# An H3 convolution block and squared-ReLU MLP: from a hand-placed order to a recorded graph with a list scheduler

## The chip, the core and the metric

The kernel runs on one NeuronCore of a Trainium2 chip. The metric is the device time of one execution, in microseconds. The core has five engines with an instruction queue each: TensorE (PE, with its weight loads shown as PEld), VectorE (DVE), ScalarE (ACT), GpSimd (POOL) and SyncE (SP), which here only issues DMA transfers. PE writes to PSUM, eight banks of 128 partitions x 512 f32; the other data lie in SBUF.

## What is computed

One block with B = 1, S = 2048 tokens, D = 640 channels, F = 1728 hidden units. Everything is f32.

```
sa, ca, ga, sb, cb, gb = six rows of (silu(c) @ w_mod)
h  = layernorm(q) * (1 + ca) + sa
ks = causal depthwise convolution of k with 4 taps
kv = ks * v
y  = long causal convolution of kv with ssm_k, per channel (FFT of length 4096) + kv * ssm_D
x  = q + ga * (h * y)
h  = layernorm(x) * (1 + cb) + sb
out = x + gb * (relu(h @ w1 + b1)^2 @ w2 + b2)
```

In this kernel the gate `ga` is row 2 of the modulation, folded into the rows for `ca` and `sa`; row 5 (`gb`) and `b2` are folded at the end.

## The kernel before

**Front: the convolution, in five blocks of 128 channels.** For each block `b`:

- `kv_load` brings k and v token-major in four pieces of 512 tokens; PE transposes them (`kv_k`, L236, and `kv_v`, L273) into PSUM; ACT and DVE apply the four taps (L238, L258) and DVE multiplies by v (L280). The product is stored to a scratch tensor `kv_d` in DRAM, and read back in another layout by `load_x` into half of the tile `p`; `load_h` reads `ssm_k` into the other half.
- `unit_a` (L380, tiles `pa`): the first stage of the FFT, 64x64 tiles of PE, four at a time; ACT copies the result to the tile `a`. Each block has eight of them, four for the filter (i = 1) and four for kv (i = 0).
- `front` (L394): the second stage, `spectrum`, for the filter (`h`) and for kv (`x`); DVE multiplies the two (L146) and POOL combines real and imaginary parts (L149, L152). In block 0 the filter's spectra are done ahead by `early_h`.
- `back` (L460, tiles `qp`): the first inverse stage, four groups a block; ACT copies to `QT`.
- `unit_t` (L523) transposes `QT`, and `unit_y` (L532) is the last inverse stage. It contracts 64 rows into 32 columns, one tile for each parity of the token tile, and fills two PSUM banks with 8 of the 16 token tiles:

```python
        for a in range(4):
            for i in range(2):
                l = slice(64 * i, 64 * i + 64)
                pe.matmul(
                    y[i][32 * a : 32 * a + 32].rearrange("p l d -> p (l d)"),
                    ca[l],
                    tss[4 * g + a][l].rearrange("p i d -> p (i d)"),
```

- `prep_a`, `prep_m`, `prep_p` make the normalised and modulated q; `gate` multiplies it with y on DVE (L146, `up<-up,KV`; in block 4 y is multiplied straight out of PSUM, L544). `finish_near` adds the first 512 tokens into the MLP's first two token tiles, `finish_add` adds the rest and stores it to the scratch tensor `x1_d`.

Beside these run the layernorm statistics of q (`stats1`) and the modulation: `part_load`, `part_scale`, `part_add`, and the column sums on PE (`mod_row`, L320; `mod_col`, L347; for row 5 `gate_sum`, L935).

**MLP.** w1 and w2 are split into a high and a low fp32r part (`w_load`, `w_high` on ACT, `w_low` on DVE). Eight tiles of 256 tokens; each runs over 14 groups of hidden units: `mlp_front` (L702; L715 and L729 in the first tile; L706 for the half-size last group), the squared ReLU (L747, L149, L749), a split into high and low (`mlp_split`, L141, L152), and `mlp_back` (L790, tiles `acc`), which runs `MLAG = 3` groups behind.

**What sets the order.** The order of each engine is the order of the calls, kept by `keep_order`. The calls of the front are written by hand: the loop over blocks calls `front`, `back`, `unit_a`, `unit_t` and `unit_y` at slots `FS(b, j)` and `GS(b, s)` listed in `UNITS`, and a table of about 100 `at(...)` lines hangs the other steps on the slots:

```python
    at(FS(1, 8), (stats1, 13), (part_add, 2, 2, pool), (part_load, 1, 0))
    at(GS(1, 1), (load_x, 2), (kv_s, 3, 0), (part_load, 1, 1))
```

All loads and stores but a few go through SP in this order (`sp_dma`, L133); each waits until the fourth one before it has landed (`OUT = 4`). PSUM is divided by tags: X (four banks: `pa`, spectra, later `acc`), Y (two: `qp`, `kt`, `y`, later `xtp`) and T (two: `t`, `mr`, some `kt` and `vt`, later the MLP's `h`).

Of the kernel before, what the change touches and what calls it, by code (L numbers as in the profile page):

```python
# [15 lines left out]
AX_X = mybir.AxisListType.X  # L16
# [5 lines left out]
NG = 16  # L22
# [5 lines left out]
MLAG = 3  # L28
OUT = 4


def _constants():
# [17 lines left out]
    for mm in range(1, 32):  # L50
# [30 lines left out]
        "ca": np.concatenate([ca, ca]).astype(f),  # L81
        "gb": gb.reshape(128, 4096).astype(f),
        "gi": gt.reshape(128, 4096).astype(f),
# [4 lines left out]
def ssm_mlp_kernel(  # L88
# [21 lines left out]
    pe, act, dve, pool, sp = nc.tensor, nc.scalar, nc.vector, nc.gpsimd, nc.sync  # L110


    def keep_order():
        info = mybir.DependencyInfo(mybir.DependencyClass.NoSync, mybir.DependencyReason.DATA)
        engines = {e.engine: None for e in (pe, act, dve, pool, sp)}
        for i in nc.cur_bb.bb.instructions:
            if i.engine in engines:
                if engines[i.engine] is not None:
                    tc.add_manual_dep(i, engines[i.engine], info, reason="order")
                engines[i.engine] = i.name  # L120
# [5 lines left out]
    kv_d = dr.tile([D, S], F32, tag="kv_d", name="kv_d")  # L126
    x1_d = dr.tile([S, D], F32, tag="x1_d", name="x1_d")
# [3 lines left out]

    def sp_dma(o, i):
        sp.dma_start(o, i)  # L133
# [5 lines left out]
    def copy(eng, o, i):  # L139
        if eng is act:  # L140
            act.activation(o, i, AF.Copy)  # L141
        else:
            eng.tensor_copy(o, i)

    def mul(eng, o, a, b):
        eng.tensor_mul(o, a, b)  # L146
# [4 lines left out]
    def sub(eng, o, a, b):  # L151
# [3 lines left out]
    WX = [sb.tile([P, 10, P], F32, tag=f"WX{i}", name=f"wx{i}") for i in range(4)]  # L155
    WE = sb.tile([P, 8, P], F32, tag="WE", name="we")
    HXS = [WX[0][:, 0:4], WX[0][:, 4:8]]
    MS = [(WX[i][:, 0:4], WX[i][:, 4:8]) for i in (1, 3)]
    TS = [WX[i][:, 4 * j : 4 * j + 4] for i in (2, 1, 3) for j in range(2)]
    WS = [  # L160
        (WE[:, 0:2], WE[:, 2:4]),
        (WE[:, 4:6], WE[:, 6:8]),
        (WX[2][:, 8:10], WX[3][:, 8:10]),
        (WX[2][:, 4:6], WX[2][:, 6:8]),
    ]
    cw = WX[0][:, 8].rearrange("p (r n) -> p r n", r=2)
    ca = WX[1][:, 8, 0:32]

    KV = sb.tile([P, 5120], F32, tag="KV", name="KV")
    KACC = [KV[:, 512 * i : 512 + 512 * i] for i in range(2)]  # L170
    KN = [
        KV[:, 1024 + 1024 * i : 2048 + 1024 * i].rearrange("p (w t d) -> p w t d", w=2, t=4)
        for i in range(4)
    ]
    K0 = sb.tile([P, 4, 512], F32, tag="UP1", name="kacc0")
    UT = KV[:, 3072:5120].rearrange("p (l d) -> p l d", l=NL)
    ktail = sb.tile([P, 2, 4], F32, tag="ktail", name="ktail")
    kover = sb.tile([P, 2, 4], F32, tag="kover", name="kover")


    ident = sb.tile([P, P], F32, tag="ident", name="ident")
    make_identity(nc, ident)
    d0 = sb.tile([P, D], F32, tag="STG", name="d0", bufs=4)
    dve.memset(d0, 0.0)
    ones = sb.tile([P, P], F32, tag="ones", name="ones")
    dve.memset(ones, 1.0)
    eps_t = sb.tile([P, 1], F32, tag="eps", name="eps_t")
    dve.memset(eps_t, EPS)
    dsm = sb.tile([P, NB, DG], F32, tag="dsm", name="dsm")
    tap = sb.tile([P, NB, 4], F32, tag="tap", name="tap")  # L190


    hsrc = ssm_k.rearrange("(g a) (n i) -> (a n) g i", a=4, i=64)
    xsrc = kv_d.rearrange("(g a) (n i) -> (a n) g i", a=4, i=64)
    qsrc = q.rearrange("(n c l) d -> c n l d", n=32, c=4)
    osrc = out.rearrange("(n c l) d -> c n l d", n=32, c=4)
    pt = {}

    def p_tile(b):
        pt[b] = sb.tile([P, 2, DG, 64], F32, tag=f"S{b % 2}", name=f"p_{b}")  # L200

    def load_h(b, n=4):
        w = DG // n
        for i in range(n):
            sp_dma(
                pt[b][:, 1, i * w : (i + 1) * w],
                hsrc[:, b * DG + i * w : b * DG + (i + 1) * w, :],
            )

    def load_x(b, n=4):  # L210
        w = DG // n
        for i in range(n):
            sp_dma(
                pt[b][:, 0, i * w : (i + 1) * w],
                xsrc[:, b * DG + i * w : b * DG + (i + 1) * w, :],
            )


    def kv_load(i):
        b, h = divmod(i, 4)  # L220
        rows = slice(h * 512, (h + 1) * 512)
        cols = slice(b * P, (b + 1) * P)
        t = KN[h % (4 if b == 0 else 2)]
        for w, src in ((0, k), (1, v)):
            sp_dma(t[:, w], src[rows, cols].rearrange("(t p) d -> p t d", p=P))

    kt = {}

    def kv_k(b, h, tag="Y"):
        acc = KACC[h % 2] if b else K0[:, h]  # L230
        t = kt[0] = ps.tile(
            [P, 512], F32, tag=tag, name=f"kt_{b}_{h}", bufs=4 if tag == "X" else 2
        )
        kn = KN[h % (4 if b == 0 else 2)]
        for j in range(4):
            pe.transpose(t[:, j * P : (j + 1) * P], kn[:, 0, j], ident)  # L236
        c = 3 if h and b else 0
        act.activation(acc[:, c:], t[:, c:], AF.Copy, scale=tap[:, b, 0:1])  # L238
        if h < 3:

            kl, ko = ktail[:, h % 2], kover[:, h % 2]
            copy(act, kl[:, 0:3], t[:, 509:512])
            if b == 0:
                return
            pool.tensor_scalar(ko[:, 0:3], kl[:, 0:3], tap[:, b, 3:4], None, op0=ALU.mult)
            for o, x, i in ((1, 2, 2), (0, 1, 2), (0, 2, 1)):
                o = ko[:, o : o + 1]
                pool.tensor_scalar(o, kl[:, x : x + 1], tap[:, b, i : i + 1], o, op0=ALU.mult, op1=ALU.add)

    def kv_s(b, h):  # L250
        acc, tk = KACC[h % 2] if b else K0[:, h], kt[0]
        if h and b:
            dve.scalar_tensor_tensor(
                acc[:, 0:3], tk[:, 0:3], tap[:, b, 0:1], kover[:, (h - 1) % 2, 0:3], op0=ALU.mult, op1=ALU.add
            )
        for t in (1, 2, 3):
            o = acc[:, t:]
            dve.scalar_tensor_tensor(  # L258
                o, tk[:, : 512 - t], tap[:, b, t : t + 1], o, op0=ALU.mult, op1=ALU.add
            )  # L260
            if h and b == 0:
                o = acc[:, :t]
                dve.scalar_tensor_tensor(
                    o, ktail[:, (h - 1) % 2, 3 - t : 3], tap[:, b, t : t + 1], o, op0=ALU.mult, op1=ALU.add
                )

    def kv_v(b, h, tag="X"):
        t = kt[1] = ps.tile(
            [P, 512], F32, tag=tag, name=f"vt_{b}_{h}", bufs=4 if tag == "X" else 2
        )  # L270
        kn = KN[h % (4 if b == 0 else 2)]
        for j in range(4):
            pe.transpose(t[:, j * P : (j + 1) * P], kn[:, 1, j], ident)  # L273
        n = 4 * b + h + 2
        if 6 <= n < 4 * NB:
            kv_load(n)

    def kv_m(b, h):
        acc = KACC[h % 2] if b else K0[:, h]
        dve.tensor_mul(acc, kt[1], acc)  # L280
        sp_dma(kv_d[b * P : (b + 1) * P, h * 512 : (h + 1) * 512], acc)


    st1 = sb.tile([P, NL, 2], F32, tag="st1", name="st1")
    rs1 = sb.tile([P, NL], F32, tag="rs1", name="rs1")
    nm1 = sb.tile([P, NL], F32, tag="nm1", name="nm1")

    qt = {}

    def dve_stats(o, t):  # L290
        s6 = sb.tile([P, 2, 6], F32, tag="s6", name="s6", bufs=2)
        for i in range(2):
            dve.bn_stats(s6[:, i], t[:, i * 320 : (i + 1) * 320])
        dve.bn_aggr(o, s6)

    def stats1(l):
        dve_stats(st1[:, l], qt[l])

    def stats1_end():
        act.activation(rs1, st1[:, :, 1], AF.Sqrt, bias=eps_t)  # L300
# [4 lines left out]
    ct = sb.tile([P, NB], F32, tag="ct", name="ct")  # L305
    sg = sb.tile([P, NB], F32, tag="sg", name="sg")
    row0 = sb.tile([P, D], F32, tag="row0", name="s1row")
    row1 = sb.tile([P, D], F32, tag="row1", name="g1row")
    cbs = sb.tile([P, 2, NB], F32, tag="cbs", name="cbs")
# [102 lines left out]

    qn = [0]
    ws = {}


    def front(b, j, early):
        n = qn[0]
# [863 lines left out]
```

## Time and profile before

| | us |
|---|---|
| median of 3 runs | 707.78 |
| the runs | 707.78, 711.22, 707.54 |
| the profiled execution | 713.03 |
| its span, first to last instruction | 711.2 |
| mean granted clock of PE | 0.965 |

The page of the profile gives the span and the busy time of each engine. A view by stretches gives for each stretch its length, the busy time of each engine with the number of instructions, the granted PE clock, the busy share of the 16 DMA engines, and GB/s. A row of the timeline reads: start, duration, engine, line, operation, out<-in, shapes, how many instructions were merged, and in brackets the idle time before it with what ended it. Starts are exact; the ends of matmuls are modelled, so the distance from one start to the next is the better price of a group. A matmul of f32 leaves two records, a transpose one. `SPq` is SP's queue of DMA issues.

### The profile page before, as it was taken

To read this page: it belongs to the slowest core of one execution; us is meant where nothing else is said; L and a number is where in the kernel's file an instruction comes from. 1 tells how busy PE (TensorE), PEld (TensorE's weight loads), DVE (VectorE), ACT (ScalarE), POOL (GpSimd) and SP (SyncE) were. 2 spreads that over 40 slices of the span, in tenths; PEclk is the share of its full clock that TensorE was granted. 3 is DMA by queue.
4 is the path that set the end of the run, shared out by engine and by line. 5 is a ranking of instruction groups with operands and counts; after the bars stand their busy time and mean duration, and the time that the engine had idled before them with its cause. 6 is when DMAs were issued, how large, how long until landed. Compare 5 with 4: busy or idle time off the path is not lost.

```text
span 711.2 us, 18076 instructions
## 1 busy us (share of the span) xinstructions
PE 647.9 (91%) x7589; PEld 583.0 (82%) x7589; DVE 417.2 (59%) x785; ACT 325.3 (46%) x683; POOL 253.0 (36%) x299
## 2 busy tenths in 40 slices
PE   6698499688969978799999999999999999999996
PEld 5687288467748858689999999999999999999995
DVE  5256646647767569768854555464555545555633
ACT  4435355568675786556533323323333333233221
POOL 1052145437966966952520300301302204103301
PEclk9999699989998999999999999999999999999999
DMA  9888977969675176338311020020020110200101
GB/s 231 247 245 197 238 194 204 234 190 214 162 201 150 51 176 151 116 104 242 104 38 38 1 75 1 1 74 1 1 75 1 38 38 1 75 1 1 38 1 38
DMA packets 109125, 74.46 MB, mean 105 GB/s; under 512 B 49266, under 2 KB 96370, under 8 KB 108788
## 3 DMA queue, kind: packets, MB, share of 16 engines
q1 hardware_dynamic: 107088, 72.87, 39.5%
q8 instruction: 60, 0.98, 0.6%
q10 hardware_dynamic: 1892, 0.43, 0.3%
q14 instruction: 21, 0.17, 0.1%
q0 software_dynamic: 64, 0.01, 0.0%
HBM read 58.86 MB, written 14.42 MB: 103 GB/s over the span
## 4 chain that ended last, share of the span: by engine, by line
PE 61%; ACT 4%; DVE 2%; DMA 2%; issue 1%; POOL 1%; DVEq 0%; POOLq 0%; ACTq 0%
PE acc L790 26%; PE h L702 22%; PE h L715 2%; PE x L394 1%; PE h L394 1%; ACT KV L493 1%; PE h L706 1%; PE qp L460 1%; PE y L532 1%; PE xtp L667 1%; DMA xp<-in_A_q_dram 1%; ACT wx L141 1%; PE gr L935 1%; PE t L523 1%; DVE w_S L152 1%
## 5 line engine op out<-in xcount | busy, mean ns | idle before, releaser
L790 PE MATMUL acc<-w_S,hring 128*128 128x320 f32 x960 | 156.7, 311 | 0.2 <-DVE hring L152 0.2
L702 PE MATMUL h<-xt,w_S 128*128 128x512 f32 (+1 forms) x770 | 149.6, 340 | 0.0
L790 PEld LDWEIGHTS acc<-w_S,hring 128*128 128x128 f32 x960 | 144.8, 188 | 4.8 <-DVE hring L152 0.7
L702 PEld LDWEIGHTS h<-xt,w_S 128*128 128x128 f32 x770 | 120.1, 189 | 14.1
L152 DVE TENSOR_TENSOR hring<-mtmp,hring 128x256 fp32r<-128x256 f32 x112 | 67.3, 601 | 69.7 <-ACT hring L141 69.7
L152 POOL TENSOR_TENSOR xt<-we,xt 128x256 fp32r<-128x256 f32 x35 | 27.4, 783 | 201.3 <-ACT xt L141 200.3
L149 DVE TENSOR_TENSOR mtmp<-h,mtmp 128x256 f32<-128x256 f32 (+1 forms) x99 | 41.9, 423 | 96.7 <-ACT mtmp L747 94.1
L747 ACT ACTIVATE mtmp<-h,b1t 128x256 f32<-128x256 f32 x91 | 43.1, 474 | 114.1 <-PE h L702 112.6
L141 ACT ACTIVATE hring<-mtmp 128x256 fp32r<-128x256 f32 x112 | 46.1, 412 | 73.9 <-DVE mtmp L749 63.2
L380 PEld LDWEIGHTS pa<-wx,p 64*64 64x64 f32 x2560 | 48.6, 154 | 23.8 <-issue 16.5
L380 PE MATMUL pa<-wx,p 64*64 64x64 f32 x2560 | 54.1, 242 | 13.6 <-DMA p<-kv_d 6.3
L141 ACT ACTIVATE a<-pa 128x512 f32<-128x512 f32 x80 | 45.2, 633 | 22.7 <-PE pa L380 22.3
L146 DVE TENSOR_TENSOR wx<-x,wx 128x512 f32<-128x512 f32 x64 | 40.8, 683 | 19.4 <-PE x L394 11.0
L394 PE MATMUL x<-a,gb 128*64 128x128 f32 x640 | 44.9, 287 | 5.0 <-DVE wx L146 2.3
L394 PEld LDWEIGHTS x<-a,gb 128*64 128x64 f32 x640 | 38.9, 145 | 6.6 <-PE h L394 3.0
L149 POOL TENSOR_TENSOR wm<-wm,wm 128x640 f32<-128x640 f32 x20 | 31.5, 1577 | 27.9 <-ACT wm L338 27.6
L749 DVE SCALAR_TENSOR_TENSOR mtmp<-mtmp 128x256 f32<-128x256 f32 x91 | 39.6, 435 | 3.1
L258 DVE SCALAR_TENSOR_TENSOR KV<-kt,tap,KV 128x511 f32<-128x511 f32 (+2 forms) x48 | 35.9, 748 | 7.9 <-ACT ktail L141 6.4
L394 PE MATMUL h<-a,gb 128*64 128x128 f32 x512 | 35.9, 284 | 2.7 <-ACT wx L141 2.7
L523 PE MATMUL t<-ident,q 128*128 128x128 f32 x160 | 25.6, 294 | 13.1 <-ACT wx L141 6.8
L394 PEld LDWEIGHTS h<-a,gb 128*64 128x64 f32 x512 | 30.2, 143 | 7.6 <-issue 3.8
L141 ACT ACTIVATE q<-qp 128x512 f32<-128x512 f32 x39 | 21.1, 593 | 32.9 <-PE qp L460 32.9
(151 smaller groups left out, 1082.7 us busy)
## 6 DMA issues: line engine op xcount, KB each, us to landing
wm<-in_w_mod_dram SPq DMA_DIRECT2D x25, 320.0 KB, 4.3
KV<-in_A_k_dram SPq DMA_DIRECT2D x20, 256.0 KB, 4.2
KV<-in_A_v_dram SPq DMA_DIRECT2D x20, 256.0 KB, 4.2
p<-in_A_ssm_k_dram SPq DMA_DIRECT2D x20, 256.0 KB, 4.9
p<-kv_d SPq DMA_DIRECT2D x20, 256.0 KB, 4.5
xp<-in_A_q_dram SPq DMA_DIRECT2D x20, 256.0 KB, 5.3
out_dram<-x SPq DMA_DIRECT2D x28, 160.0 KB, 2.6
w1s<-in_B_w_dram SPq DMA_DIRECT2D x13, 320.0 KB, 4.0
```

The costliest lines, as they stand in the source:

```text
L141: act.activation(o, i, AF.Copy)
L146: eng.tensor_mul(o, a, b)
L149: eng.tensor_add(o, a, b)
L152: eng.tensor_sub(o, a, b)
L258: dve.scalar_tensor_tensor(o, tk[:, : 512 - t], tap[:, b, t : t + 1], o, op0=ALU.mult, op1=ALU.add)
L380: pe.matmul(t[e][64 * r : 64 * r + 64, g].rearrange("p m d -> p (m d)"), pt[b][l, i, 8 * q + g, :], cw[l, r], start=True, stop=True,)
L394: pe.matmul(t[64 * a : 64 * a + 64, s + r], gb[:, g, r, a], AX[b][i][:, 2 * g + a], start=True, stop=True,)
L523: pe.transpose(t[:, i], x, ident)
L702: pe.matmul(*x, start=(b == 0 and x is both), stop=(b == NB - 1 and x is both))
L747: act.activation(r, h[:, 1], AF.Identity, bias=b1t[:, f : f + 1])
L749: dve.scalar_tensor_tensor(r, r, 0.0, r, op0=ALU.max, op1=ALU.mult)
L790: pe.matmul(acc[2 * s + i], h[:, a, s * P : (s + 1) * P], w[:, y, i * 320 : (i + 1) * 320], start=(f == 0 and ti == 0), stop=(f == NF - 1 ...
```

## The change

The kernel's calls no longer issue instructions. They record nodes in a graph, with the buffers that they read and write, a rough cost, and for each buffer the places where it may lie. `Graph.order` then runs a list scheduler in the source: at every moment each engine takes the ready node of highest priority (length of the longest path behind it, plus hand-set offsets by kind and block in `BIAS`) whose buffers find a free place; it keeps account of SP's four transfers in flight, of PE's instruction supply (a matmul counts 4 entries, 256 entries in 4 us), and of a port that DVE and POOL share. `emit` issues the nodes in that order. `FS`, `GS`, `at`, `AFTER`, `UNITS` and `MLAG` go.

```diff
+    def order(self, lag=0.1, pelag=0.2, patience=0.0, trace=None):
...
+                    for k, (pr, i) in enumerate(ready[e]):
+                        if nodes[i].lock and port[0] > t + 1e-9 and port[1] != e:
+                            continue
+                        got = place(nodes[i])
+                        if got is not None:
+                            pick = k
+                            break
...
+                    if e == "PE":
+                        ent += n.entries
+                        if ent >= 256:
+                            end = max(end, block + 4.0)
+                            block, ent = end, ent - 256
...
+    g.bias = BIAS
+    g.emit(g.order())
     keep_order()
```

PSUM is eight single banks; most tiles of the front may take any of them, `qp` any of four, and in the MLP `acc` has banks 0 to 3, `h` and `xtp` banks 4 to 7:

```diff
+    bank = [ps.tile([P, 2, 512], F32, tag=f"PS{i}", name=f"ps{i}") for i in range(4)]
...
+    ANY = (0, 1, 2, 3, 4, 5, 6, 7)
+    ONE = (6, 7)
+    MAIN = (0, 1, 2, 3)
+    SIDE = (4, 5)
...
+    KVB, PAB, XB, QB = ANY[::-1], ANY, ANY, ANY[2:6][::-1]
+    TB, YB, XTB, HB, ACCB = ANY[::-1], ANY[::-1], SIDE + ONE, SIDE + ONE, MAIN
```

The last inverse stage contracts both parities at once. The constant `ca` becomes block diagonal, 128 rows by 64 columns with half of it zeros, `gi` is permuted to suit, and a call of `unit_y` makes one quarter of the tokens (4 of 16 token tiles) in one bank, with two matmuls of 512 columns:

```diff
-        "ca": np.concatenate([ca, ca]).astype(f),
+        "ca": np.kron(np.eye(2), ca).astype(f),
...
+    def unit_y(b, l):
...
+            for h in range(2):
+                mm(
+                    y[64 * h : 64 * h + 64].rearrange("p l d -> p (l d)"),
+                    ca,
+                    ts[h].rearrange("p l d -> p (l d)"),
+                    True,
+                    True,
+                    hold=[d],
+                )
...
+        if raw:
+            copy(act, d, y)
+            mul(dve, d, d, u)
+            U[b, l] = d
+        else:
+            mul(dve, u, y, u)
```

`raw` holds for blocks 0 and 1; in blocks 2 to 4 the product with the normalised q `u` is read straight from PSUM. The products on POOL after the spectra are now in place (`wr` and `wi` lie in `m0`), with a small tile `keep` for the two rows of the first group. The counts of the other matmuls and transposes, the transfers, and the arithmetic of the MLP are those of before.

In the order that results, SP's queue begins with the eight k and v loads of block 0. The reload `load_x` of block 0 is issued as transfers 27 to 30 (20 to 23 before), behind the eight k and v loads and two stores of block 1. The spectra of a block are interleaved with `qp`, `t` and `y` of the block before it:

```
... pa2 pa2 pa2 pa2 pa2 pa2 h2 h2 vt3 x2 x2 vt3 vt3 mr1 y1 h2 x2 t1 t1 kt4 h2 x2 kt4 h2 x2 ...
```

(a name is one group on PE, with its block; `mr1` is the product of modulation row 1). In the MLP's first tile PE runs 45 parts of `mlp_front`, five to a hidden group, ahead of the first part of `mlp_back`.

More of the change, by code (lines that the diff above doesn't have):

```diff
@@ L109, in ssm_mlp_kernel @@
     nc = tc.nc
-    pe, act, dve, pool, sp = nc.tensor, nc.scalar, nc.vector, nc.gpsimd, nc.sync
+    engines = {"PE": nc.tensor, "ACT": nc.scalar, "DVE": nc.vector, "POOL": nc.gpsimd, "SP": nc.sync}
     def keep_order():
         info = mybir.DependencyInfo(mybir.DependencyClass.NoSync, mybir.DependencyReason.DATA)
-        engines = {e.engine: None for e in (pe, act, dve, pool, sp)}
+        last = {e.engine: None for e in engines.values()}
         for i in nc.cur_bb.bb.instructions:
[L117 to L120, printed above, removed]
+            if i.engine in last:
+                if last[i.engine] is not None:
+                    tc.add_manual_dep(i, last[i.engine], info, reason="order")
+                last[i.engine] = i.name
     sb = ctx.enter_context(tc.tile_pool(name="sb", bufs=1))
@@ new lines, in ssm_mlp_kernel, with one, make @@
+    UT = [part(lambda: KV, 3072 + 512 * i, (f"KN{2 + i // 2}{'ab'[i % 2]}",)) for i in range(4)]
+    KVALL = (("KA0", "KA1") + tuple(f"KN{i}{h}" for i in range(4) for h in "ab"), lambda s, d, n: sb.tile(s, d, tag="KV", name=n))
+    bank = [ps.tile([P, 2, 512], F32, tag=f"PS{i}", name=f"ps{i}") for i in range(4)]
+    def one(i):
+        def make(s, d, n):
+            return shaped(bank[i // 2][: s[0], i % 2, : int(np.prod(s[1:]))], s)
+        return ((f"B{i}",), make)
+    banks = [one(i) for i in range(8)]
@@ new lines, in act_dma, with cost @@
+    def act_dma(o, i, run):
+        g.add("ACT", 0.06, (nc.scalar.dma_start, "dma", (o, i), {}), [x for x in (o,) if isinstance(x, View)],
+              [x for x in (i,) if isinstance(x, View)], dma=moved(o, i, run))
+    def cost(engine, op, args, kw):
+        o = args[0]
+        n = o.ix.size if op != "bn_stats" else args[1].ix.size
+        ins = [a for a in args[1:] if isinstance(a, View)]
+        deep = any(a.buf.psum for a in ins)
+        if engine == "ACT":
+            given = any(isinstance(kw.get(x), View) for x in ("scale", "bias"))
+            return (0.38 if given else 0.19) + 0.00083 * n
+        if engine == "DVE":
+            if op == "bn_stats":
+                return 0.15 + 0.001 * n
+            if op in ("tensor_mul", "tensor_add", "tensor_sub") and not deep:
+                return 0.1 + 0.00115 * n
+            if op == "bn_aggr":
+                return 0.21
+            return 0.19 + 0.0011 * n
+        if n < 200 or op == "tensor_copy":
+            return 0.36
+        return 0.1 + 0.0023 * n
@@ new lines, in ssm_mlp_kernel, with __init__, __getattr__, call @@
+    class Engine:
+        def __init__(self, name):
+            self.name = name
+        def __getattr__(self, op):
+            def call(*args, hold=(), **kw):
+                ins = [a for a in (*args[1:], *kw.values()) if isinstance(a, View)]
+                fn = getattr(engines[self.name], op)
+                flat = not any(a.buf.psum for a in ins)
+                lock = self.name == "POOL" or (self.name == "DVE" and flat and (len(ins) > 1 or op == "tensor_copy") and args[0].ix.size > 64)
+                g.add(self.name, cost(self.name, op, args, kw), (fn, op, args, kw), [args[0]], ins, hold=hold, lock=lock)
+            return call
@@ new lines, in ssm_mlp_kernel, with mm, turn @@
+    act, dve, pool = Engine("ACT"), Engine("DVE"), Engine("POOL")
+    def mm(o, a, b, start, stop, hold=()):
+        n = 2 if (isinstance(b, View) and b.buf.dtype == F32R) else 4
+        ins = [x for x in (a, b) if isinstance(x, View)]
+        g.add("PE", 0.0, (nc.tensor.matmul, "matmul", (o, a, b), dict(start=start, stop=stop)), [o], ins, entries=n, hold=hold)
+    def turn(o, x, hold=()):
+        g.add("PE", 0.0, (nc.tensor.transpose, "transpose", (o, x, ident), {}), [o], [x], entries=4, hold=hold)
@@ L178, in ssm_mlp_kernel @@
[L178 to L190, printed above, removed]
+    kv_d = g.buf("kv_d", [D, S], F32, [])
@@ new lines, in mod_col, with dve_stats @@
+    def mod_col(j, dst, plus):
+        a = mod_sum(j)
+        g.key = ("mr", j)
+        t = psum(f"mc_{j}", (P, NB), ONE)
+        with g.as_one(1.8):
+            for b in range(NB):
+                mm(t[:, b : b + 1], a[:, b * P : (b + 1) * P], ones[:, 0:1], True, True)
+        dve.tensor_scalar(dst, t, float(plus), None, op0=ALU.add)
+    st1, rs1, nm1 = small("st1", (P, NL, 2)), small("rs1", (P, NL)), small("nm1", (P, NL))
+    def dve_stats(o, t):
+        s6 = sbuf("s6", (P, 2, 6), [whole("s6a"), whole("s6b")])
+        for i in range(2):
+            dve.bn_stats(s6[:, i], t[:, i * 320 : (i + 1) * 320])
+        dve.bn_aggr(o, s6)
@@ L239, in kv_k @@
         if h < 3:
[L241 to L251, printed above, removed]
+            kl = tails[b, h] = sbuf("ktail", (P, 4), [whole("kta"), whole("ktb")])
@@ new lines, in spectra @@
+    def spectra(name, b, i, j, hold=()):
+        t = psum(f"{name}_{b}_{j}", (P, 4, P), XB, name)
+        with g.as_one(0.88):
+            if name == "x" and b:
+                g.group.deps.add(hnode[0])
+            hnode[0] = g.group.id
+            for n in range(2):
+                for r in range(2):
+                    for a in range(2):
+                        mm(t[64 * a : 64 * a + 64, 2 * n + r], gb[:, 2 * j + n, r, a], AX[b][i][:, 2 * (2 * j + n) + a], True, True, hold=hold)
+        return t
@@ L422, in front @@
         else:
[L423 to L431 removed]
+            h = sbuf(f"hx_{b}_{j}", (P, 4, P), [work[i] for i in HXW], line="hx")
```

1654 lines of the change are left out of this document (819 added, 835 removed), and 8 rows, old and new, of tables (BIAS, UNITS).

## Prediction

> **What bounds the kernel now.** The head of the page comes first: TensorE (PE) is the busiest engine by far.
>
> ```profile
> span 711.2 us, 18076 instructions
> ## 1 busy us (share of the span) xinstructions
> PE 647.9 (91%) x7589; PEld 583.0 (82%) x7589; DVE 417.2 (59%) x785; ACT 325.3 (46%) x683; POOL 253.0 (36%) x299
> ```
>
> 91% hides two very different halves. I cut the span where the spectra of each of the five channel blocks begin (x of block 0, then h of blocks 1 to 4), where the MLP begins, and where its last contraction ends, and asked for the busy time of each stretch.
>
> ```profile
> core 0: us, PE busy (x) PEld busy (x) DVE busy (x) ACT busy (x) POOL busy (x), PEclk, DMA share, GB/s
> 0.00:37.04 37.04, 23.37 (x641) 20.64 (x641) 12.92 (x28) 16.62 (x31) 3.25 (x13) 0.94 0.91 238
> 37.04:94.52 57.48, 45.78 (x916) 38.21 (x916) 34.84 (x66) 25.55 (x50) 18.22 (x39) 0.86 0.87 221
> 94.52:155.72 61.20, 50.81 (x1013) 42.54 (x1012) 36.91 (x70) 36.32 (x67) 29.36 (x43) 0.92 0.79 203
> 155.72:217.00 61.28, 51.13 (x1015) 42.28 (x1007) 42.41 (x62) 45.89 (x94) 43.05 (x48) 0.92 0.83 197
> 217.00:266.77 49.77, 45.27 (x978) 38.18 (x970) 32.90 (x43) 37.14 (x77) 40.24 (x38) 0.93 0.52 123
> 266.77:310.18 43.41, 37.75 (x481) 30.53 (x479) 36.91 (x58) 24.96 (x54) 30.84 (x34) 1.00 0.52 142
> 310.18:703.50 393.32, 392.92 (x2565) 370.00 (x2564) 217.44 (x456) 138.86 (x313) 86.14 (x83) 1.00 0.14 39
> 703.50:711.20 7.70, 0.84 (x6) 0.57 (x4) 2.83 (x6) 0.00 (x0) 1.92 (x2) 0.84 0.29 85
> ```
>
> From 310.18 to 703.50 PE is busy 392.92 of 393.32 us at full clock: the MLP is pure PE work, and only fewer matmuls could shorten it. Before 310.18 PE idles, and its granted clock is 0.86 to 0.94, while the DMA engines are 79 to 91% busy up to 217 us. How much of those 310.18 us is work? The timeline of PE, from start to start in stretches at full speed, gives a price for each group:
>
> ```profile
> 154.71 1.09 PE L532 MATMUL y<-wx,wx 64*32 64x512 f32 x16
> 155.72 1.09 PE L394 MATMUL h<-a,gb 128*64 128x128 f32 x16
> 156.65 1.04 PE L394 MATMUL x<-a,gb 128*64 128x128 f32 x16
> 157.52 1.04 PE L394 MATMUL h<-a,gb 128*64 128x128 f32 x16
> ...
> 179.56 2.06 PE L460 MATMUL qp<-gi,we 64*128 64x128 f32 x32
> 181.55 1.34 PE L320 MATMUL mr<-wm,ones 128*128 128x320 f32 x4
> 182.82 2.06 PE L460 MATMUL qp<-gi,wx 64*128 64x128 f32 x32
> 184.81 1.16 PE L380 MATMUL pa<-wx,p 64*64 64x64 f32 x64
> 185.90 0.66 PE L236 MATMUL kt<-ident,KV 128*128 128x128 f32 x4
> 186.39 0.60 PE L523 MATMUL t<-ident,q 128*128 128x128 f32 x4
> 186.92 1.16 PE L380 MATMUL pa<-wx,p 64*64 64x64 f32 x64
> ```
>
> So y 1.01 (154.71 to 155.72), a spectrum 0.87, qp 1.99, a pair of 128x320 products 1.27, pa 1.09, four k or v transposes 0.49, four t transposes 0.53. The source has 40 groups of k/v transposes (19.6), 40 pa (43.6), 80 spectra (69.6), 20 qp (39.8), 40 t (21.2), 10 y (10.1), and 16 products of 128x320, two column sums and ten MLP transposes (my estimate 14 from the same rows): 218 us. So 310 - 218 = 92 us of the front are lost on PE to waits and low clock. That is all that a better order can win; the rest of the span it cannot touch.
>
> By the same prices, work and loss up to each cut are: x of block 0, 18 done, 19 lost; h of block 1, 56 and 39; block 2, 99 and 56; block 3, 142 and 75; block 4, 180 and 86; MLP, 218 and 92. Some 18 to 20 us go at each of the first boundaries, and these rows show how:
>
> ```profile
> 85.72 1.95 PE L532 MATMUL y<-wx,wx 64*32 64x512 f32 x14 [4.66 <-DVE KV L258]
> 87.61 3.59 PE L380 MATMUL pa<-wx,p 64*64 64x64 f32 x128
> ...
> 132.15 1.98 PE L380 MATMUL pa<-wx,p 64*64 64x64 f32 x64 [3.93 <-DMA p<-kv_d]
> ```
>
> In the first, y waits for a PSUM bank that DVE is still reading for the k convolution. In the last, pa waits for the reload of kv. And the same 64 pa records that took 1.09 at 184.81 take 1.98 after that 3.93 us gap: a gap is paid twice. The Trainium skill, "TensorE: Matmul & The Clock Gate", Part 1, says that PE's clock falls to half after an idle window of about 3.4 us and returns after one as busy; the rows agree (1.98 against 1.09), and shortening gaps is worth more by it than their length.
>
> **The change, part by part.**
>
> *The last stage.* Before, unit_y uses 64x32 tiles: 16 records, two banks, 1.01 us. After, two matmuls per bank contract 128 rows (half of the new constant is zeros) into 64 columns. The nearest row is the spectrum: the same 128*64 tiles, 8 matmuls of 128 columns in 0.87 us, as many streamed columns as 2 of 512. So 20 x 0.87 = 17.4 for 10.1: PE work rises by 7.3, to 225. Bounds: nothing, if the zero half were free, and +10.1, if a bank costs a whole 1.01. The Trainium skill, "TensorEngine Tiling (Array Packing)", Theoretical Speedup, gives up to 2x for splitting rows when the contraction is 64 or less, so it speaks against this edit: by it the cost would be the full doubling, 10.1. The gating by u is read straight from PSUM for three blocks, which saves DVE copies and ACT copies; both engines are under 75% busy in every stretch but the 85% of DVE from 266.77, so I count nothing, and if that cover fails the sign is a gain.
>
> *What y buys.* A y group now yields one quarter of the tokens, and the first MLP tile needs only the first quarter of block 4. The remaining y, t and gate products (about 14 us of PE) can lie over its normalisation.
>
> *The order on PE and on the DMA queue.* Built instructions stand exactly as the list scheduler set them. I counted what lies ahead of each milestone. The loads matter most: 4 may be in flight and the queue is in order, so a load lands no sooner than the bytes ahead of it allow. The kv reloads (load_x) before were issued here:
>
> ```profile
> 24.54 2.99 SPq L133 DMA_DIRECT2D p<-kv_d  x4
> ...
> 126.69 4.95 SPq L133 DMA_DIRECT2D p<-kv_d  x4
> ...
> 170.56 4.67 SPq L133 DMA_DIRECT2D p<-kv_d  x4
> 218.67 3.96 SPq L133 DMA_DIRECT2D p<-kv_d  x4
> ```
>
> With 5.8, 28.2, 37.4 and 46.4 MB ahead of blocks 0, 2, 3 and 4 in its queue (summed from the transfers' shapes), before ran at 236, 223, 219 and 212 GB/s. After, the last reload of each block has 9.4, 14.2, 29.3, 42.4 and 46.7 MB up to it. At 220 GB/s these land at 43, 64, 133, 193 and 212 us; at the 238 of the first stretch at 40, 60, 123, 178 and 196. So block 0 starts 3 to 6 us later than 37.04 (eight loads and two stores of block 1 now stand ahead of its reload), but block 1 is loaded some 16 to 20 us earlier than its pa used it (from 87.61, the row above), and the boundaries overlap: h and x of the next block are interleaved with qp, t and y of this one.
>
> Ahead of h of block 2 PE has 96 us of work, ahead of h of block 3 138 us: 39 k/v groups 19.1, 64 half pa groups 34.9, 48 spectra 41.8, 12 qp 23.9, 16 t 8.5, 7 y 6.1, 6 products 3.8. If the DMA paces both, plus 3 us for the last pa and its eviction, h of block 2 starts at 126 to 136 (155.72 before) and of block 3 at 181 to 196 (217.00 before); lost by then 43 to 58, not 75. Afterwards the reload of block 4 (196 to 212) comes well before its use. Before lost 17 from there to the MLP (75 to 92); with y, t and qp of block 3 over the spectra of block 4 I take 10, with 0 and 17 as ends. MLP start: 225 + 43 + 10 = 278 to 225 + 58 + 10 = 293. I take 288, nearer to the slow end, because the stretches from 37 to 217 us ran at 197 to 221 GB/s.
>
> *Shared PSUM banks and buffer places.* They add no instruction; a wait for a bank is what they can add, from nothing to rival one below.
>
> *The MLP.* The matmuls are those of before, and the two accumulator pairs still use four banks, h and transposes four. The new order runs nine hidden groups of the first tile ahead of the first contraction, while DVE splits weights; the last weight loads stand behind the final store of block 4's rows. From 0 to 6 us; I take 1, since after the first tile PE always has hidden groups in hand. The end (7.70) stays.
>
> Sum: 288 + 393.3 + 1 + 7.7 = 690 against a span of 711.2. The profiled execution took 713.03 in all, 1.8 outside its span and 5.3 over the median of 707.78, so 690 + 1.8 - 5.3 = 687 for the median. With the ends (an MLP start of 268 with 43 and nothing more lost; 300 with 58 and 17, and 6 in the MLP) the likeliest case alone spans 667 to 704.
>
> **The rivals.**
>
> *One, slower: shared banks turn late evictions into PE stalls.* Every PE group now takes whichever of eight banks was expected free when the order was laid, and PE is in order. The y row above is that wait in today's kernel: 4.66 us, and then the low clock. If it strikes once at each of the 20 y groups at about half that, 2 us, 40 us come back; from 21 us on the gain is gone. Price: 687 + 40, less 8 that DMA waits would have cost anyway, gives 719. For it: the clock penalty and the fixed order. Against it: today's tags confine stages to two banks, and eight give more slack.
>
> *Two, the same: the boundaries are paced by the evictions.* If ACT, DVE and POOL chains set them (ACT and POOL are busy 75% and 70% from 155.72 to 217.00), the earlier reloads bring nothing, and the 7 us won in the tail (17 lost before, 10 after) are spent on y (7) and the later start (4): 704 to 711.
>
> *Three, faster: short gaps, full clock.* The clock column says 0.06 to 0.14 of each of the first five stretches, 23 us in all, was withheld. If the interleaving leaves no gap long enough to cool PE, and the DMA runs at 238, about half of the 23 comes off the 278: the MLP starts near 266, and 687 - 22 = 665. The Trainium skill, "TensorE: Matmul & The Clock Gate", Part 1, would make the full clock the outcome once no gap exceeds its window; the trace shows only that a gap of 3.93 us costs it.
>
> That the order might not be kept is excluded by the built order; that y is a win on its own is not forecast.
>
> **How the numbers follow.** Forecast 0.62, rival one 0.18, two 0.08, three 0.12. Half a per cent, 3.5 us, is about what this measurement can tell from no change. Forecast and rival three are faster: 0.74; rival two same: 0.08; rival one slower: 0.18. From 664 to 716 some 0.13 is left out: the upper half of rival one and the lower edge of three.
>
> **What would show it.** In the profile after: h of block 3 starting between 181 and 196 us and the MLP between 278 and 293; y in groups of four records at about 0.87; a first reload at 40 to 43; DMA share above 0.85 up to 190; MLP stretch 393 to 400. Wrong if PE's idle time ahead of y or t is put to evictions (rival one), if h of block 3 starts after 205 with the reload long landed (rival two), or if the clock column stays at 1.00 from block 1 on (rival three).

## The result, and the profile after

| | before | after |
|---|---|---|
| median, us | 708.13 (4 runs, 707.54 to 711.22) | 774.83 (4 runs, 771.35 to 776.13) |
| ratio, 95% interval | 1 | 1.0925 (1.0876 to 1.0973) |
| span of the profiled execution, us | 711.2 | 774.3 |

The changed kernel is 9% slower, where 3% faster was forecast and 716 us was the upper end of the range. The head of its page, in answer to that of before:

```profile
span 774.3 us, 17837 instructions
## 1 busy us (share of the span) xinstructions
PE 667.8 (86%) x7509; PEld 583.5 (75%) x7509; DVE 391.0 (50%) x780; ACT 326.8 (42%) x678; POOL 253.7 (33%) x316
```

There are fewer instructions; DVE is busy 26 us less, and ACT and POOL are within 2 us of before. PE's busy time grew by 20 us, of which 15.6 fall in the MLP, where its matmuls are those of before (408.48 against 392.92), and its idle time grew by 43. The view by stretches, cut at the same places (x of block 0, h of blocks 1 to 4, start and end of the MLP):

```profile
core 0: us, PE busy (x) PEld busy (x) DVE busy (x) ACT busy (x) POOL busy (x), PEclk, DMA share, GB/s
0.00:51.70 51.70, 31.26 (x674) 27.78 (x674) 23.96 (x48) 19.41 (x37) 7.00 (x25) 0.80 0.87 219
51.70:87.43 35.73, 28.49 (x780) 25.50 (x777) 14.93 (x23) 16.90 (x32) 18.98 (x37) 0.95 0.81 217
87.43:155.40 67.97, 54.95 (x1050) 45.27 (x1044) 37.61 (x85) 37.22 (x69) 28.55 (x46) 0.97 0.85 213
155.40:218.06 62.66, 49.62 (x974) 39.25 (x970) 41.66 (x66) 40.61 (x83) 36.38 (x48) 0.95 0.74 174
218.06:278.70 60.64, 45.62 (x930) 37.19 (x930) 27.99 (x45) 37.37 (x74) 38.96 (x36) 0.92 0.54 122
278.70:338.71 60.01, 49.37 (x553) 36.88 (x551) 41.16 (x65) 38.63 (x79) 40.12 (x43) 1.00 0.49 138
338.71:768.15 429.44, 408.48 (x2571) 371.69 (x2569) 201.95 (x448) 136.67 (x309) 82.78 (x82) 1.00 0.11 32
768.15:774.30 6.15, 0.00 (x0) 0.00 (x0) 1.69 (x4) 0.00 (x0) 0.90 (x2) 0.82 0.38 107
```

Two things are lost. The MLP begins at 338.71, not at 310.18. And the MLP itself takes 429.44 us with 2571 matmul records, where before took 393.32 for 2565, at a clock of 1.00 and with the DMA engines 89% idle. That second loss is the telling one: none of the reasons that make the front hard (transfers, cold clock, long chains between engines) is there. Here is one hidden group of the MLP in the timeline of all engines (PE's weight loads left out; what is in brackets is the idle time before the row and what ended it):

```profile
453.37 0.85 PE L375 MATMUL ps<-xt,w_S 128*128 128x512 f32 x4
454.25 0.47 ACT L375 ACTIVATE mtmp<-ps,b1t 128x256 f32<-128x256 f32 x1 [1.29 <-PE ps L375]
454.78 0.96 PE L375 MATMUL ps<-xt,w_S 128*128 128x256 f32 x4 [0.56 <-ACT mtmp L375]
455.85 0.42 DVE L375 TENSOR_TENSOR mtmp<-ps,mtmp 128x256 f32<-128x256 f32 x1 [2.37 <-PE ps L375]
...
456.33 0.62 PE L375 MATMUL ps<-xt,w_S 128*128 128x256 f32 x2 [0.59 <-DVE mtmp L375]
456.79 0.59 PE L375 MATMUL ps<-w_S,hring 128*128 128x320 f32 x3
```

The ten matmuls of one group fill one bank. ACT and DVE here read the group before it, which lies in the next bank. Yet they take turns: PE does four, ACT waits for these and reads, PE waits for ACT and does four more, DVE waits for those and reads, PE waits for DVE and does the last two. 3.42 us (453.37 to 456.79) for a group that by the forecast needed no wait at all. The built program says why: the group lies in bank 4; its fifth matmul waits for ACT's read of bank 5, and its ninth for DVE's read of bank 5.

In the source the eight banks are four tiles, `bank = [ps.tile([P, 2, 512], F32, ...) for i in range(4)]`. The waits are not written in the kernel; the layer below puts semaphores in from what touches each tile. For the waits of PE instructions on ACT or DVE in the built programs, the table gives how many name an instruction that touches only the same tile and not the same data:

| built program | waits of PE on ACT and DVE | of these, same tile but other data |
|---|---|---|
| after | 409 | 181 |
| after, with eight tiles of one bank (first experiment) | 459 | 2 |

ACT and DVE have such waits on PE as well. This is theory A: **two banks in one tile count as one thing to wait for, so an engine that works in one bank waits for the users of its neighbour.** The rivals: B, the scheduler's fixed order is bad by itself; C, PE has more work (the fuller last stage, instruction supply). Later D was added: the plan takes loads for landed too early.

### The profile page after: what moved, and what is told of

Read it like the earlier page. It is cut to its first block, busy times and chain, and to the rows that moved or that the text cites. A ratio compares the mean times of both kernels' runs of the same rounds, so it can differ in the third digit from the quotient of the medians.

```text
span 774.3 us, 17837 instructions
## 1 busy us (share of the span) xinstructions
PE 667.8 (86%) x7509; PEld 583.5 (75%) x7509; DVE 391.0 (50%) x780; ACT 326.8 (42%) x678; POOL 253.7 (33%) x316
## 5 line engine op out<-in xcount | busy, mean ns | idle before, releaser
L375 PE MATMUL ps<-xt,w_S 128*128 128x512 f32 (+1 forms) x935 | 174.0, 332 | 14.7 <-ACT mtmp L375 6.6
L375 PEld LDWEIGHTS ps<-xt,w_S 128*128 128x128 f32 x935 | 139.4, 188 | 39.2 <-ACT mtmp L375 12.1
L375 PE MATMUL ps<-w_S,hring 128*128 128x320 f32 x648 | 108.6, 312 | 0.2
L375 PE MATMUL ps<-a,gb 128*64 128x128 f32 x1280 | 83.0, 284 | 21.2 <-DVE wx L375 10.5
L375 PEld LDWEIGHTS ps<-w_S,hring 128*128 128x128 f32 x648 | 98.2, 188 | 2.1 <-DVE mtmp L375 0.7
L375 PEld LDWEIGHTS ps<-a,gb 128*64 128x64 f32 x1280 | 72.9, 142 | 33.2 <-DVE wx L375 12.1
L375 ACT ACTIVATE mtmp<-ps,b1t 128x256 f32<-128x256 f32 (+1 forms) x112 | 51.6, 472 | 93.4 <-PE ps L375 55.3
L375 ACT ACTIVATE hring<-mtmp 128x256 fp32r<-128x256 f32 x74 | 30.7, 415 | 108.8 <-PE ps L375 101.5
L375 POOL TENSOR_TENSOR wx<-wx 128x256 f32<-128x256 f32 x80 | 60.3, 774 | 41.6 <-DVE wx L375 40.8
L375 PE MATMUL ps<-cst,p 64*64 64x64 f32 x2560 | 54.9, 236 | 17.2 <-issue 5.0
L375 PE MATMUL ps<-w_S,w_W 128*128 128x320 f32 x312 | 51.4, 311 | 0.4 <-DVE mtmp L375 0.2
```

Source lines behind the costliest of these rows:

```text
L375: fn(*real, **{k: a.real() if isinstance(a, View) else a for k, a in kw.items()})
```

## The experiments

**Eight tiles of one bank.** The scheduler's order is untouched, instruction for instruction:

```diff
-    bank = [ps.tile([P, 2, 512], F32, tag=f"PS{i}", name=f"ps{i}") for i in range(4)]
+    bank = [ps.tile([P, 512], F32, tag=f"PS{i}", name=f"ps{i}") for i in range(8)]
...
-            return shaped(bank[i // 2][: s[0], i % 2, : int(np.prod(s[1:]))], s)
+            return shaped(bank[i][: s[0], : int(np.prod(s[1:]))], s)
```

> The changed kernel with each PSUM bank a tile of its own; the order of every engine stays as the scheduler laid it. Theory A (the pairs): in the changed kernel two banks are one tile, and a wait for the one is also put on users of the other, so PE and the evicting engines take turns where they should overlap. Then this gives back the 35 us of the MLP (its stretch falls from 428 to 393 to 398 us) and most of the growth of the front, 690 to 720 us in all. Theory B (the order): the list scheduler's fixed order is what costs, so 765 to 780, with the same idle times on PE. Theory C (PE's work: the fuller last stage, instruction supply): also 765 to 780.

Measured: 705.31 (7 runs), ratio to before 0.9927 (0.9896 to 0.9958), span 705.4. Two changed lines take 69 us off the kernel, and it is then slightly faster than the kernel before. The view by stretches (columns as above; 35.81 is where the first pa of block 0's kv starts, 74.54, 135.85 and 193.06 where h of blocks 1 to 3 starts), and a hidden group with the evictions of its neighbour beside it:

```profile
0.00:35.81 35.81, 20.99 (x416) 19.19 (x417) 18.77 (x41) 16.72 (x32) 7.00 (x25) 0.95 0.99 256
35.81:74.54 38.73, 32.27 (x1032) 29.76 (x1032) 19.33 (x31) 19.89 (x37) 18.86 (x37) 0.96 0.98 262
74.54:135.85 61.31, 54.33 (x1048) 45.05 (x1043) 35.45 (x78) 38.40 (x72) 28.55 (x46) 0.94 0.89 224
135.85:193.06 57.21, 49.23 (x976) 39.76 (x971) 45.88 (x75) 40.37 (x82) 36.26 (x49) 0.91 0.83 200
...
300.76:699.50 398.74, 396.24 (x2571) 371.41 (x2569) 204.29 (x448) 136.14 (x308) 86.04 (x83) 1.00 0.12 34
```

```profile
412.59 1.91 PE L375 MATMUL ps<-xt,w_S 128*128 128x512 f32 x10
412.68 0.47 ACT L375 ACTIVATE mtmp<-ps,b1t 128x256 f32<-128x256 f32 x1 [0.50 <-DVE w_W L375]
413.19 0.42 DVE L375 TENSOR_TENSOR mtmp<-ps,mtmp 128x256 f32<-128x256 f32 x1 [0.54 <-ACT mtmp L375]
...
414.33 0.60 PE L375 MATMUL ps<-w_W 128*128 128x320 f32 x3
```

Ten matmuls in one row, 1.74 us from start to start, while ACT and DVE read beside them. Against the changed kernel the front is 38.0 us shorter (338.71 to 300.76), the MLP 30.7 (429.44 to 398.74) and the end 0.25: all of the 68.9. The waits of PE, first the changed kernel's, then those of this run (us in total, times, longest):

```profile
PE ps L375 <- ACT wx L375: 16.3, 14, 3.9
PE ps L375 <- DVE wx L375: 14.9, 17, 3.1
PE ps L375 <- ACT mtmp L375: 7.7, 19, 0.6
...
PE ps L375 <- DVE mtmp L375: 7.3, 15, 0.7
...
PE ps L375 <- ACT a L375: 6.3, 8, 1.2
```

```profile
PE ps L375 <- ACT wx L375: 9.6, 5, 4.1
...
PE ps L375 <- DVE wx L375: 2.9, 2, 2.2
```

The many short waits go (`mtmp` in the MLP, `DVE wx` at the spectra's products, `ACT a` at pa). A few long ones stay: those for `ACT wx`, and two each for DVE at the taps on k (`DVE kacc` 4.7 us, `DVE KV` 4.6, the longest of them 4.1 and 4.3). Those for `ACT wx` come up again below.

**One half of the banks at a time.** The same edit for banks 4 to 7 alone (hidden groups and transposes in the MLP), then for banks 0 to 3 alone (the accumulators).

> The changed kernel with banks 4 to 7 as tiles of their own and banks 0 to 3 still two pairs. In the MLP banks 0 to 3 hold only the accumulators, which are read once a token tile, and banks 4 to 7 the hidden groups and transposes. Theory A: the MLP stretch falls to 393 to 400 us and the front gains only a part, 715 to 745 in all. Theories B and C: 765 to 780.

> The changed kernel with banks 0 to 3 as tiles of their own and banks 4 to 7 still two pairs, the reciprocal of the run before. Theory A: the MLP stretch stays at 420 to 430 us, the front gains a part, 745 to 770 in all. Theories B and C: 765 to 780 with the front unchanged as well.

First and last matmul rows of the MLP, first with banks 4 to 7 split, then with banks 0 to 3 split:

```profile
323.14 0.73 PE L375 MATMUL pq<-xt,w_S 128*128 128x256 f32 x3
...
721.42 2.21 PE L375 MATMUL ps<-w_KA,hring 128*128 128x320 f32 x14
```

```profile
311.61 0.77 PE L375 MATMUL ps<-xt,w_S 128*128 128x256 f32 x3
...
735.65 2.21 PE L375 MATMUL pq<-w_KA,hring 128*128 128x320 f32 x14
```

Banks 4 to 7 split: 731.10 (4 runs), ratio 1.0305 (1.0250 to 1.0360); the MLP takes 400.5 (323.14 to 723.63), the front 323.1. Banks 0 to 3 split: 746.18 (4 runs), ratio 1.0513 (1.0483 to 1.0542); the MLP takes 426.3, the front 311.6. The MLP's loss lies in the pairs 4-5 and 6-7, as theory A has it, and the front's in both halves. B and C expected 765 to 780 from all three runs and are out as causes of the 69 us.

**The other way round: the kernel before, paired.** If the pairs cost, they must also cost in the order written by hand.

```diff
+    class Pairs:
+        """Two banks of a tag lie in one tile; a use takes the next bank of its tag."""
...
+    ps = Pairs(ps)
```

> The kernel before in its own order, but with its eight PSUM banks as four tiles of two banks (the four X banks as two pairs, the Y and the T banks as one each); nothing else is changed. Theory A: the added waits strike this order too, in the front at each pair of spectra and in the MLP at each hidden group, 730 to 790 us. Theory B, and C: the grouping of banks into tiles costs nothing, 705 to 712.

786.17 (4 runs), ratio 1.1087 (1.1021 to 1.1154). But this form went round the banks of a tag in turn, which is not what the pool of the kernel before does, so buffers came to lie in other banks as well: two changes at once. It was replaced by one in which every buffer has the bank that the pool had given it.

> The kernel before in its own order and with every PSUM buffer in the very bank that it had, only that banks 0 and 1, 2 and 3, 4 and 5, 6 and 7 are one tile each. Theory A (the pairs): each engine now also waits for users of the neighbouring bank, in the front at the spectra and in the MLP at the hidden groups, 730 to 790 us. Theory B (the scheduler's order) and C (PE's work): nothing changes, 705 to 712.

781.27 (4 runs), ratio 1.0999 (1.0940 to 1.1057). The instructions, their order on each engine and the banks are those of before; the waits are not. PE has 390 waits on ACT and DVE in place of 619, and 326 of the 390 are for the neighbour alone.

Both paired forms also leave something out. In the kernel before, PE holds y back in three places until DVE has applied the taps to a piece of k in the same bank, 11.4 us in all (the y row at 85.72 in the prediction is one). In the paired forms DVE applies these taps, for one piece each of blocks 2, 3 and 4, only after y has overwritten the bank, so their output is not that of the block, and their front is that of a kernel without these three waits.

Its stretches, where before took 310.18 and 393.32, and the longest waits of PE (its lines are 27 further down than those of before: L421 is the spectra, L550 is `t`, L407 is `pa`). In before the same waits came to 2.3 (spectra on DVE), 6.8 (`t` on ACT), under 2.3 (`pa` on ACT) and 2.7 us (spectra on ACT):

```profile
0.00:366.60 366.60, 263.40 (x5022) 212.38 (x5023) 185.05 (x323) 188.00 (x369) 165.33 (x214) 0.91 0.63 159
366.60:771.27 404.67, 399.02 (x2569) 370.47 (x2567) 218.23 (x457) 139.90 (x316) 86.00 (x83) 1.00 0.13 38
```

```profile
PE ps L421 <- DVE wx L173: 20.5, 19, 1.8
PE ps L550 <- ACT wx L168: 15.7, 17, 1.4
PE ps L407 <- ACT a L168: 14.1, 18, 1.8
PE ps L421 <- ACT wx L168: 8.5, 6, 3.1
```

The front loses 56 us and the MLP, which comes after the three places, 11. Theory A holds in both kernels, though what the three places do to the 56 is not separated. The number of waits does not set their price: in the MLP PE has 145 for the neighbour alone here and 90 in the changed kernel, which loses 31 by them. That the MLP loses less here because the hand-written order puts contractions between two hidden groups, so that the evictions are mostly over, I only argue.

**Other partners.** The changed kernel with banks 0 and 4, 1 and 5, 2 and 6, 3 and 7 in a tile (`bank[i % 4][..., i // 4, ...]`).

> The changed kernel with four tiles of two banks as it has them, and its order, but other partners: banks 0 and 4, 1 and 5, 2 and 6, 3 and 7 share a tile. Now an accumulator of the MLP shares with a hidden group. Theory A (waits for users of the partner bank): the stretches change with the partners; the contractions now wait for the evictions of hidden groups, so the MLP takes longer than the 429 us of the changed kernel, 440 to 520, and the whole 780 to 870. If wide tiles cost by themselves, whoever the partner is: 770 to 780 with the MLP at 425 to 433.

734.55 (5 runs), ratio 1.0342 (1.0312 to 1.0372). Width alone is not it: the same four tiles of two banks, other partners, 40 us less. But my figure for theory A pointed the wrong way: I had 440 to 520 for the MLP and 780 to 870 in all. The MLP fell to 411.1:

```profile
321.72 0.77 PE L375 MATMUL ps<-xt,w_S 128*128 128x256 f32 x3
...
730.59 2.21 PE L375 MATMUL ps<-w_KA,hring 128*128 128x320 f32 x14
```

An accumulator shared with a hidden group costs less than two hidden groups in a tile. Again it is not the number of waits: PE has 78 for the neighbour alone in this MLP, and 78 in that of the run with banks 0 to 3 split, which took 426.3. That the second are always in use one straight after the other, as in the row by row reading above, is my explanation; no run separates it further.

**The last stage by halves.** With eight tiles, each bank of y filled by four matmuls of 64 rows into 32 columns, without the zeros of the block diagonal constant; the order is kept.

```diff
             for h in range(2):
-                mm(
-                    y[64 * h : 64 * h + 64].rearrange("p l d -> p (l d)"),
-                    ca,
-                    ts[h].rearrange("p l d -> p (l d)"),
...
+                for a in range(2):
+                    k = slice(64 * a, 64 * a + 64)
+                    o = 64 * h + 32 * a
+                    mm(
+                        y[o : o + 32].rearrange("p l d -> p (l d)"),
+                        ca[k, 32 * a : 32 * a + 32],
+                        ts[h][k].rearrange("p l d -> p (l d)"),
...
```

> The kernel with eight single banks, order unchanged, but the last stage goes back to tiles of 64x32: each bank is filled by four matmuls of 64 rows into 32 columns instead of two of 128 rows into 64, so the zero half of the constant is not streamed. If the term of the prediction is right (0.88 a group against some 0.5, 20 groups), PE's work falls by 7 to 8 us. If y lies on the path that sets the end, the whole falls from 705 to 696 to 700; if PE only waits longer elsewhere, 702 to 706.

707.23 (12 runs), ratio 0.9947 (0.9920 to 0.9974), not to be told from the 0.9927 with eight tiles. The reason is not that y is hidden: its price did not fall. The same group of y in both timelines, its first two rows and the row after it (eight tiles, then by halves):

```profile
168.52 0.64 PE L375 MATMUL ps<-we,cst 128*64 128x512 f32 x1
168.52 0.64 PE L375 MATMUL ps<-wx,cst 128*64 128x512 f32 x1
...
169.53 0.55 PE L375 MATMUL ps<-ident,q 128*128 128x128 f32 x3
```

```profile
167.87 0.62 PE L375 MATMUL ps<-we,cst 64*32 64x512 f32 x2
167.88 0.62 PE L375 MATMUL ps<-wx,cst 64*32 64x512 f32 x2
...
168.86 0.66 PE L375 MATMUL ps<-ident,q 128*128 128x128 f32 x4
```

1.01 with the zeros, 0.99 without. The rows of a group begin within 0.01 us of each other, so its matmuls run side by side: two of 128 rows, or four of 64. The kernel before had the 16 records of eight 64x32 matmuls, about 0.6 us each, in the same 1.01 (154.71 to 155.72), and they filled two banks. So the run could not test what 7 us of PE work are worth here: filling one bank at a time, the small tiles gain nothing over the zeros.

**The plan's transfers.** With single banks PE still has a few long waits. One of them, with the row of ACT that explains it:

```profile
238.61 0.49 ACT L375 ACTIVATE KV<-xp,nm,rs 128x128 f32<-128x128 f32 x1 [6.36 <-DMA xp<-in_A_q_dram]
```

```profile
212.61 1.98 PE L375 MATMUL ps<-a,gb 128*64 128x128 f32 x16 [2.24 <-DVE wx L375]
...
239.64 1.79 PE L375 MATMUL ps<-wx,cst 128*64 128x512 f32 x2 [4.07 <-ACT wx L375]
...
281.97 1.50 PE L375 MATMUL ps<-ident,q 128*128 128x128 f32 x12 [1.93 <-DVE q L375]
...
293.52 0.65 PE L375 MATMUL ps<-ident,q 128*128 128x128 f32 x4 [1.65 <-ACT we L375]
```

ACT stood 6.36 us before an instruction whose load had not landed; the copy that y needs was queued behind it, and PE waited 4.07. The scheduler prices a load of 256 KB at 0.98 us, 268 GB/s. The stretches above show 256 and 262 up to 74.54 us, where the DMA engines are 98 to 99% busy, and 224 and 200 after it, where they are 89 and 83% busy; so the price is near the rate of the first two and too low for the later ones. Theory D: with a truer price the order would not put such instructions in front.

```diff
-        return n / run * (0.0095 + 4.1e-5 * run) / 16
+        return n / run * (0.0095 + 4.1e-5 * run) / 16 * 1.15
```

> The kernel with eight single banks, and the scheduler prices every transfer 1.15 times as high, so that the order of all engines is laid anew; nothing else is changed. In the run with single banks the longest idle times of PE in the front (3.8 us at 101, 4.3 at 146, 4.1 at 240) follow an instruction of ACT or DVE that waited 3 to 6 us for a load at the head of its queue. Theory D (the plan takes loads for landed too early): these go, 690 to 701 us. Rival: the offsets in BIAS fit the old price, and the new order loses elsewhere what it wins, 703 to 720.

718.87 (6 runs), ratio 1.0109 (1.0055 to 1.0164): slower than with the old price, with the MLP beginning at 308.31. The rival has it so far. So the offsets in `BIAS` were searched anew for this price, twice, and replaced as a whole:

> Eight single banks, transfers priced 1.15 times as high in the scheduler, and the offsets of BIAS searched anew for that price (they had been kept in the run with slower transfers in the plan, which came out at 719 with the first MLP matmul at 308 us). Theory D (the rest of the front's loss comes from a plan that takes loads for landed too early): with offsets that fit, the MLP begins at 288 to 297 us and the whole takes 690 to 699. Rival: the front's loss is work and bytes, which no order shifts, 703 to 712.

> The same as the run before with the offsets of another search, which lays the second and third block in another order. Both theories as there: 690 to 699 by theory D, 703 to 712 by the rival. If the two differ by over 1%, what counts is the one order and not the price of the transfers.

702.50 (6 runs), ratio 0.9902 (0.9874 to 0.9931), and 698.84 (6 runs), ratio 0.9852 (0.9827 to 0.9877). The second beats both kernels, by 1.5% and 9.8%:

```profile
296.03 0.64 PE L375 MATMUL ps<-xt,w_S 128*128 128x256 f32 x2
...
688.68 2.21 PE L375 MATMUL ps<-w_KA,hring 128*128 128x320 f32 x14
```

Its MLP begins at 296.03 (300.76 with the old price and offsets) and takes 394.9; the first's begins at 301.41 and takes 394.7. The second falls where theory D put it; the first, 702.50, lies between the two ranges, with its MLP starting later than theory D has it. Price and offsets were changed together and the two differ by half a per cent, so theory D is neither shown nor excluded: what is shown is that offsets found for one price do not carry over to another (705 with the old price, 719 with the new one and the old offsets, 699 and 703 with new ones).

## Why the prediction was wrong

The step that failed is the paragraph on shared PSUM banks: "They add no instruction; a wait for a bank is what they can add, from nothing to rival one below." I priced that wait as a wait for one's own bank, with eight banks to choose from, and never asked what the program's unit of waiting is. The diff, which I quoted, has it: four tiles of two banks. Point by point:

- *Sum.* Forecast span 690, measured 774.3. Of the 84.3 us, 68.9 are the pairs (38.0 in the front, 30.7 in the MLP, 0.25 at the end, by the run with eight tiles). The other 15.4: the MLP starts 12.8 later than 288, takes 4.4 more than 394.3, and the end is 1.8 shorter. Without the pairs, 705.3 would have lain inside the range of 664 to 716, 2.7% over the 687, but with 0.7% gained and not the 3% forecast.
- *The order on PE and the DMA queue.* The reload of block 0 is SP's transfers 30 to 33, not 27 to 30; the 9.4 MB up to its end are right. The spectra of block 0, forecast at 40 to 43, start at 43.80 with eight tiles and at 51.70 with the pairs. With eight tiles h of block 2 starts at 135.85 (forecast 126 to 136) and h of block 3 at 193.06 (181 to 196), so this working held, at its slow end. With the pairs they start at 155.4 and 218.06, as late as before (155.72 and 217.00). The DMA share is 0.99 to 0.83 up to 193 us in the one, and falls to 0.74 in the other.
- *The tail.* From h of block 3 to the MLP I took 10 us lost, with 17 as the end. With eight tiles it is 107.7 us for 87 of work, 20.7 lost. This term was mis-sized by 10.7, which is most of the 12.8; the rows at 212.61 to 293.52 above show 9.9 of it as waits.
- *The MLP.* "From 0 to 6 us; I take 1, since after the first tile PE always has hidden groups in hand." With eight tiles it is 398.74 against 393.32, 5.4, inside the bounds. With the pairs it is 36.1: work in hand does not help an engine that is made to wait in the middle of a group.
- *The last stage.* Forecast 0.87 a group, measured 0.86 (258.63 to 259.49 with eight tiles) to 1.01 at full clock, so 7 to 10 us more in all against 7.3. The Trainium skill, "TensorEngine Tiling (Array Packing)", Theoretical Speedup, gives up to 2x for splitting the rows, and by it the cost would have been 10.1. The trace agrees at its upper end: 1.01 us for one bank now, 1.01 for two banks with eight tiles of 64x32 before. The split gains only where it fills the array: four such tiles took 0.99 for one bank.
- *Rival one.* The family was right, its place and price were not: it was to strike at the 20 y groups with 2 us each and give 719. Ahead of y PE waits 16.0 us in ten places, with 3.93 as the longest (row below); with eight tiles 9.4 in four. So y has 6.6 us of what the pairs cost; they strike more at the spectra, at pa and at the hidden groups of the MLP, mostly for half a microsecond to a few, and give 775. The check that was to show it, PE idle ahead of y for an eviction, would have pointed at y alone, and the longest such wait left with eight tiles (4.07 ahead of y at 239.64) follows a late load.

```profile
166.35 1.11 PE L375 MATMUL ps<-wx,cst 128*64 128x512 f32 x1 [3.93 <-ACT wx L375]
```

- *Rivals two and three.* The clock was 0.92 to 0.97 from 51.70 to 278.70 us, and 0.91 and 0.94 in the rows shown with eight tiles, not full, so three is out. Two (704 to 711, paced by evictions) is near what the kernel with eight tiles does, for another reason: the spectra did start earlier, and the tail gave it back.

## What to carry to other kernels

Read how buffers are cut into tiles as closely as what is computed: if waits are placed by tile, two buffers in one tile cost a wait at every meeting of their users, without an instruction in the diff. The Trainium skill, "Perfetto Trace Analysis", Matmuls, says that independent matmul groups should rotate through different PSUM banks so that one's eviction lies over the next one's matmuls; this case adds that the banks must also be different tiles (705 against 775 us with the same rotation). Counting such waits does not price them (145 cost the MLP of the paired kernel before 11 us, 90 cost that of the changed kernel 31): look at what each one interrupts. And where a loss shows in a stretch that has no transfers, no cold clock and no new work, look at a single group there first: PE's ten matmuls cut into four, four and two told more than any sum over the span.

## What was not expected of the hardware

Filling one bank of 512 columns took PE the same time with two matmuls of 128 rows by 64 columns (1.01 us) and with four of 64 rows by 32 columns (0.99 us), while the kernel before filled two banks with eight of 64 by 32 in 1.01 us. The matmuls of a group ran side by side in each case, and 512 columns took about 1 us whether two, four or eight lay beside each other. So the half of the constant that is zeros cost nothing against four small tiles, and a factor of two against eight.
